# Attention and gated feed-forward on one core: constants as planned tasks, masks from five patterns, and new due times for the planner

## The chip, the cores and the metric

The kernel runs on one core of a Trainium2 chip. The core has TensorE (PE in the profile, with its weight loads as PEld), VectorE (DVE), ScalarE (ACT), GpSimd (POOL) and SyncE (SP, which here only issues DMAs). The metric is the device time of one launch in microseconds, the median of several runs.

## The reference

Eight batches, eight heads, 576 positions, head size 64. Heads 0 to 3 attend to the last 32 positions, heads 4 to 7 to every fourth position of the last 128. The result of all heads, 576 x 512 per batch, goes through a gated feed-forward with 1024 inner channels.

```python
scores = scale * np.matmul(q, k.transpose(0, 1, 3, 2))
rel = pos[:, None] - pos[None, :]
mask_plain = (rel >= 0) & (rel < window)                     # window 32
mask_dil = (rel >= 0) & (rel < window * dilation) & (rel % dilation == 0)   # dilation 4
...
attn = np.exp(scores - max) ; attn = attn / (sum + 1e-09)
x = matmul(attn, v)                       # heads side by side: (batch, 576, 512)
h = np.maximum(x @ w_in, 0.0)             # 512 -> 1024
conv_out = sum over k in 0..2 of conv_w[k] * h shifted by k - 1 along the sequence
gate = 1.0 / (1.0 + np.exp(-conv_out))
return h * gate @ w_out                   # 1024 -> 512
```

## The kernel before

**Attention.** Two heads make a pair; pairs 0 and 1 of a batch are plain, pairs 2 and 3 dilated. The scores of a pair are computed only inside the bands: 128 partitions by nine blocks of 64 columns, in three banks of a PSUM buffer called `att`, with 72 or 80 small matmuls (line 264). `att` has one buffer, used by a pair first for the scores (S) and later for the values (V, line 318). Between S and V stand on DVE and ACT: mask, maximum, exponential, sum, division, and a transpose to `pt` (line 307). After V, ACT writes the rounded result `xa` (line 368) and DVE the remainder `xb` (line 384); only then is `att` free.

**Eased pairs.** The eight pairs of batches 0 and 1 (`EASED = 8`) get their mask from TensorE: ahead of the scores three matmuls (line 253) with the weights `ones` (an identity in bf16) copy a mask from `mask_sb` to the three banks, and the scores are added on top. Then come a maximum on DVE (lines 274 to 278) and nine exponentials with sums on ACT (line 284). In later batches DVE adds the mask from `mask_sb` (lines 289 and 292), takes the maximum (294), subtracts it (296), ACT takes one exponential (298) and DVE sums (300).

**Masks.** `kinds_sb` holds five patterns of 64 columns, loaded by a DMA on ACT's queue. `mask_sb` holds for each kind ten blocks of 64 and is filled from the patterns by five ACT copies (lines 522 to 526). `ident` is an identity in fp32 that POOL makes; `minus` and `ones` are made from it by ACT (lines 516 and 517).

**Feed-forward.** A batch has a first product (line 402, into `mm`, and for half of batch 0's units into `nn`) in 16 units (eight chunks of 128 channels, two halves of 288 positions), each of four tasks of three matmuls (hi x hi, hi x lo, lo x hi). ACT applies the relu into `h` (line 409; three buffers), then the middle tap (420); DVE adds two taps (414), ACT takes the sigmoid (425), DVE multiplies (427), ACT rounds to `ga` (429) and DVE takes the remainder `gb` (431), the last gate step of a chunk. The second product (line 444, into `nn`) has eight units of eight tasks, one task for each chunk; ACT copies it out (451) and SP stores it.

**Weights.** They come as float64 and are turned into two fp32r parts by ACT and DVE (lines 477 to 512): an absolute value on ACT, five steps on DVE, and then either three matmuls on TensorE with `ident` and `minus` (lines 499 to 501, the nine "summed" ones) or two more DVE steps (506 and 512). POOL issues their DMAs (line 470) into the three buffers `out`.

**Order.** A planner written in Python sets the order of all engines when the kernel is built. Each piece of work is a task with an engine, a cost, a due time, the tasks it follows and the buffers it uses. The planner walks through time; of the tasks that could start within 0.25 of the earliest one on an engine it takes the one due first. The due times of attention pairs (`PAIR`), of first products, gates and second products (`DUE`) and of weights (`WI`, `WO`) are numbers; from batch 2 on they are those of one batch moved by `PERIOD`. The engines then run their instructions strictly in the planned order. What is set up before the planner (the mask DMA, the identity, the mask copies, the zeros at the edges of `h`) is not in the plan, and is put in order by the framework.

## Time and profile before

| what | value |
|---|---|
| median of 3 runs | 547.44 us (547.39 to 547.52) |
| profiled execution | span of 546.0 us from its first to its last instruction; the page gives no other time of it |
| PE busy | 514.2 us, 94% |
| DVE, ACT busy | 405.1 us (74%), 301.0 us (55%) |
| first matmul | at 9.96 us |
| granted TensorE clock, mean | 0.991 |

The busy time of matmuls is modelled at their ends, so a busy PE can still hold short waits. A row of the timeline gives start, duration, engine, line and instruction, with the idle time ahead of it and what ended it in brackets. A row of the waits gives the total, the number and the longest. Stages are given from the span's start. A unit's pace on PE is read from starts, not from the sum of durations, since matmuls overlap.

### The profile page before, as it was taken

How to read it: one execution, taken by the hardware profiler on the slowest of the kernel's cores; microseconds unless marked ns; L12 is line 12 of the kernel's file. 1: busy time of each engine (PE TensorE's matmuls, PEld its weight loads, DVE VectorE, ACT ScalarE, POOL GpSimd, SP SyncE). 2: the span in 40 equal slices, each digit the busy share in tenths (PEclk: the TensorE clock that was granted, in tenths of full speed). 3: DMA queues.
4: the chain of work that ended last, by engine and by line, in shares of the span. 5: the costliest groups of instructions: out<-in, count | busy, mean ns of one | idle time of the engine just before them, and what ended most of it. 6: DMA issues, size and time to landing. Idle time of an engine off the chain costs nothing.

```text
span 546.0 us, 18894 instructions
## 1 busy us (share of the span) xinstructions
PE 514.2 (94%) x8508; PEld 487.9 (89%) x8508; DVE 405.1 (74%) x692; ACT 301.0 (55%) x681; POOL 10.2 (2%) x29
## 2 busy tenths in 40 slices
PE   1668999999989999999999999999999999999997
PEld 1356888999979999999999999999999999999997
DVE  1878899998997389856998289856998289856920
ACT  3647799655742487237742577227743576237721
POOL 1100000000000000000000000000000000000000
PEclk9969999999999999999999999999999999999999
DMA  6656634022235102440045102440045102200011
GB/s 250 220 185 226 191 98 136 5 82 97 73 118 176 33 22 77 151 151 22 1 165 165 57 13 78 153 147 23 1 161 176 49 14 78 99 26 22 1 44 43
DMA packets 16959, 52.29 MB, mean 96 GB/s; under 512 B 1888, under 2 KB 3056, under 8 KB 16880
## 3 DMA queue, kind: packets, MB, share of 16 engines
q1 hardware_dynamic: 14400, 42.60, 23.7%
q0 software_dynamic: 2336, 8.41, 4.7%
q8 instruction: 66, 1.08, 0.8%
q10 hardware_dynamic: 144, 0.08, 0.1%
q14 instruction: 13, 0.11, 0.1%
HBM read 41.66 MB, written 9.44 MB: 94 GB/s over the span
## 4 chain that ended last, share of the span: by engine, by line
PE 80%; ACT 10%; DVE 7%; DMA 1%; issue 1%; POOL 0%; ACTq 0%; DVEq 0%; POOLq 0%
PE nn L444 36%; PE mm L402 32%; PE att L318 6%; PE att L264 5%; ACT s L284 4%; DVE c L414 2%; DMA out<-in_w_in_dram 1%; ACT c L420 1%; ACT h L409 1%; DVE m L274 1%; ACT c L425 1%; DVE c L427 1%; ACT L425 0%; DVE pt L307 0%; ACT w1a L477 0%
## 5 line engine op out<-in xcount | busy, mean ns | idle before, releaser
L414 DVE SCALAR_TENSOR_TENSOR c<-h,conv_sb,c 128x576 f32<-128x576 f32 x128 | 103.9, 815 | 37.8 <-ACT c L420 36.6
L409 ACT ACTIVATE h<-mm 128x288 f32<-128x288 f32 x120 | 48.9, 409 | 51.9 <-PE mm L402 51.7
L451 ACT COPY out<-nn 128x288 f32<-128x288 f32 x64 | 25.3, 398 | 71.0 <-PE nn L444 66.8
L427 DVE TENSOR_TENSOR c<-c,h 128x576 f32<-128x576 f32 x64 | 48.0, 754 | 14.4 <-ACT c L425 12.8
L318 PEld LDWEIGHTS att<-pt,v 32*64 32x64 f32 x2944 | 38.6, 135 | 14.7 <-ACT s L284 5.1
L318 PE MATMUL att<-pt,v 32*64 32x64 f32 (+2 forms) x2944 | 42.4, 230 | 8.4 <-ACT s L284 4.0
L420 ACT ACTIVATE c<-h,conv_sb 128x576 f32<-128x576 f32 x64 | 49.5, 775 | 1.1
L425 ACT ACTIVATE c<-c 128x576 f32<-128x576 f32 x64 | 43.4, 679 | 5.2 <-DVE c L414 4.4
L402 PE MATMUL mm<-x2a,wi 128*128 128x288 f32 x144 | 40.6, 297 | 0.7 <-ACT h L409 0.7
L402 PE MATMUL mm<-x0a,wi 128*128 128x288 f32 x144 | 40.4, 296 | 0.0
L402 PE MATMUL mm<-x3a,wi 128*128 128x288 f32 x144 | 40.3, 296 | 0.0
L402 PE MATMUL mm<-x1a,wi 128*128 128x288 f32 x144 | 40.3, 295 | 0.0
L444 PE MATMUL nn<-g0a,wo 128*128 128x288 f32 x128 | 37.3, 306 | 0.2
L264 PE MATMUL att<-qk 64*32 64x64 f32 x2432 | 35.4, 232 | 1.8 <-DVE s L292 1.4
L444 PE MATMUL nn<-g2a,wo 128*128 128x288 f32 x128 | 36.7, 302 | 0.0
L444 PE MATMUL nn<-g1a,wo 128*128 128x288 f32 x128 | 36.5, 300 | 0.0
L444 PE MATMUL nn<-g3a,wo 128*128 128x288 f32 x128 | 36.4, 299 | 0.0
L264 PEld LDWEIGHTS att<-qk 64*32 64x32 f32 x2432 | 29.7, 109 | 7.4 <-issue 4.1
L444 PE MATMUL nn<-g4a,wo 128*128 128x288 f32 x128 | 36.3, 299 | 0.0
L444 PE MATMUL nn<-g6a,wo 128*128 128x288 f32 x128 | 36.2, 299 | 0.0
L402 PE MATMUL mm<-x4a,wi 128*128 128x288 f32 x128 | 35.8, 295 | 0.0
L402 PE MATMUL mm<-x5a,wi 128*128 128x288 f32 x128 | 35.8, 295 | 0.0
(170 smaller groups left out, 1498.5 us busy)
## 6 DMA issues: line engine op xcount, KB each, us to landing
qk<-in_qk_d_dram SPq DMA_DIRECT2D x16, 664.0 KB, 4.7
qk<-in_qk_p_dram SPq DMA_DIRECT2D x16, 592.0 KB, 4.1
out_dram<-out SPq DMA_DIRECT2D x28, 288.0 KB, 2.1
v<-in_v_p_dram SPq DMA_DIRECT2D x16, 384.0 KB, 3.7
v<-in_v_d_dram SPq DMA_DIRECT2D x16, 384.0 KB, 3.5
out<-in_w_in_dram POOLq DMA_DIRECT2D x8, 512.0 KB, 4.0
out<-in_w_out_dram POOLq DMA_DIRECT2D x8, 512.0 KB, 3.9
out_dram<-out SPq DMA_DIRECT2D x8, 144.0 KB, 1.8
```

Source lines behind the costliest of these rows:

```text
L264: nc.tensor.matmul(sc.t[quad * 32:quad * 32 + 32, bank, c * W:c * W + W], q, k, start=i == 0 and not eased, stop=i == len(parts) - 1, skip ...
L274: last = plan.add("DVE", 0.68, due + 1.5, lambda: nc.vector.tensor_reduce(out=m.t.rearrange("p (h a) -> p h a", h=2)[:, :, 0:4], in_=banks ...
L284: nc.scalar.activation(out=s.t[:, i, :], in_=sc.t[:, bank, c * W:c * W + W], func=AF.Exp, scale=SCALE, bias=m.t[:, i:i + 1], accum_out=z.t ...
L318: nc.tensor.matmul(tv.t[hd * 64:hd * 64 + 64, bank, o:o + n], v.t[quad * 32:quad * 32 + 32, block // 2, block % 2 * 64:block % 2 * 64 + 64 ...
L402: nc.tensor.matmul(ps.t[:, 0:HALF], wi[jw][fc][:, k * 128:k * 128 + 128], x[k].t[jx][:, hf * HALF:hf * HALF + HALF], start=(k == 0 and i = ...
L409: relu.append(plan.add("ACT", 0.4, due + 1.6 * u + 1.6, lambda fc=fc, hf=hf, ps=ps: nc.scalar.activation(out=h[fc].t[:, 1 + hf * HALF:1 + ...
L414: nc.vector.scalar_tensor_tensor(out=c[fc].t, in0=h[fc].t[:, k:S + k], scalar=conv_sb[:, k, fc:fc + 1], in1=c[fc].t, op0=ALU.mult, op1=ALU ...
L420: t = plan.add("ACT", 0.777, d, lambda fc=fc: nc.scalar.activation(out=c[fc].t, in_=h[fc].t[:, 1:S + 1], func=AF.Copy, scale=conv_sb[:, 1, ...
L425: t = plan.add("ACT", 0.686, d + 1.0, lambda fc=fc: nc.scalar.activation(out=c[fc].t, in_=c[fc].t, func=AF.Sigmoid), [t], [c[fc]], "sigmoid")
L427: t = plan.add("DVE", 0.755, d + 1.5, lambda fc=fc: nc.vector.tensor_tensor(out=c[fc].t, in0=c[fc].t, in1=h[fc].t[:, 1:S + 1], op=ALU.mult ...
L444: nc.tensor.matmul(ps.t[:, 0:HALF], wo[jw][2 * dm + k // 4][:, k % 4 * 128:k % 4 * 128 + 128], g[k].t[jg][:, hf * HALF:hf * HALF + HALF], ...
L451: outs.append(plan.add("ACT", 0.4, out_due + 3.3 + 3.3 * u, lambda hf=hf, ps=ps, o=o: nc.scalar.copy(out=o.t[:, hf * HALF:hf * HALF + HALF ...
```

## The change

The constants become tasks of the plan with very early due times, and the mask copies tasks with due time 70 (`MASKS`); only the mask DMA stays ahead of the plan, as ACT's first instruction. The scores follow the task that makes `ones`. In eased pairs TensorE no longer reads `mask_sb`: it builds each bank from the patterns themselves, which it reads repeated. In the planner, engines begin at times of their own (`FIRST`) instead of 0, a load on SP takes 0.3 longer, and a first S 0.4 longer in batch 0. All due times are replaced, now with own numbers for every batch.

```diff
+DUE = {
+    0: (-0.8, 5.8, -44.0),
...
+}
+PAIR = {
+    0: (-206.5, -338.2, -201.8, -179.4),
+    1: (-72.2, -148.2, -76.5, -59.2),
...
+}
+MASKS = 70.0
...
-    LATENCY = {"DVE": 0.05, "ACT": 0.05, "SP": 2.0, ...
+    LATENCY = {"DVE": 0.05, "ACT": 0.05, "SP": 2.3, ...
+    FIRST = {"SP": 0.75, "POOL": 1.0, "PE": 4.5, "ACT": 2.5}
...
-        at = 0.0
+        at = self.FIRST.get(t.engine, 0.0)
...
-                for bank, (c0, c1) in enumerate(((0, 256), (320, 576), (256, 320))):
-                    nc.tensor.matmul(sc.t[:, bank, 0:c1 - c0], ones, mask_sb[:, kind, c0:c1], start=True, stop=True,
-                                     skip_group_check=True)
+                own = ((0, 1), (2, 3)), ((2, 4),), ((1, 1),)
+                if kind == 1:
+                    own = ((3, 1), (2, 3)), ((3, 1), (2, 3)), ((4, 1),)
+                for bank, runs in enumerate(own):
+                    c = 0
+                    for i, n in runs:
+                        nc.tensor.matmul(sc.t[:, bank, c * W:(c + n) * W].rearrange("p (a k) -> p a k", k=W), ones,
+                                         kinds_sb[:, i, :].unsqueeze(1).to_broadcast([128, n, W]),
+                                         start=c == 0, stop=True, skip_group_check=True)
+                        c += n
...
-        last = plan.add("PE", (0.8, 0.92)[kind] + (0.5 if eased else 0.0), due, scores, [lq], [qk, sc, s], "S")
+        last = plan.add("PE", (0.8, 0.92)[kind] + (0.5 if eased else 0.0) + (0.4 if b == 0 else 0.0), due, scores, [lq, made], [qk, sc, s], "S")
...
-    nc.scalar.dma_start(out=kinds_sb, in_=mask)
-    make_identity(nc, ident)
-    nc.scalar.mul(out=minus, in_=ident, mul=-1.0)
-    nc.scalar.copy(out=ones, in_=ident)
+    made = plan.add("POOL", 0.6, -1e4, lambda: make_identity(nc, ident))
+    made = plan.add("ACT", 0.29, -1e4, lambda: nc.scalar.copy(out=ones, in_=ident), [made])
+    plan.add("ACT", 0.29, -1e4, lambda: nc.scalar.mul(out=minus, in_=ident, mul=-1.0), [made])
...
+    masked = [None, None]
+    for kind, (rest, own) in enumerate(((0, lambda: nc.scalar.copy(out=slot_masks[0][:, 0:5:4, :], in_=kinds_sb[:, 0:2, :])),
+                                        (1, lambda: nc.scalar.copy(out=slot_masks[1][:, 0:6:5, :], in_=spread(3, 2))))):
+        masked[kind] = plan.add("ACT", 0.72, MASKS, lambda k=kind: nc.scalar.copy(out=slot_masks[k], in_=spread(2, 10)))
+        masked[kind] = plan.add("ACT", 0.29, MASKS, own, [masked[kind]])
...
     with tc.manual_schedule():
+        nc.scalar.dma_start(out=kinds_sb, in_=mask)
         for t in plan.order():
             t.run()
```

The change moves instructions on all engines. Three places matter here. The first is ACT at the program's beginning. Before:

```order
L522 COPY mask_sb<-kinds_sb 128x640
L524 COPY mask_sb<-kinds_sb 128x640
L523 COPY mask_sb<-kinds_sb 128x2x64
L525 COPY mask_sb<-kinds_sb 128x2x64
L526 COPY mask_sb<-kinds_sb 128x64
L477 ACTIVATE w0a<-out_151 128x512
L516 ACTIVATE minus<-ident 128x128
L517 CAST ones<-ident 128x128
L284 ACTIVATE s_104,z_110<-att_160,m_107 128x64 x9
```

The same place now:

```order
L531 COPY mask_sb<-kinds_sb 128x640 x2
L529 COPY mask_sb<-kinds_sb 128x2x64
L530 COPY mask_sb<-kinds_sb 128x2x64
L533 COPY mask_sb<-kinds_sb 128x64
L515 CAST ones<-ident 128x128
L516 ACTIVATE minus<-ident 128x128
L477 ACTIVATE w0a<-out_151 128x512
L284 ACTIVATE s_104,z_110<-att_160,m_107 128x64 x9
```

`ones` and `minus` have moved ahead of the first weight (`w0a`); the five mask copies still stand ahead of them.

The second place is TensorE at the program's beginning, where `qk` is a pair's queries and keys, `pt` its transposed weights. Before:

```order
L253 LDWEIGHTS ones
L253 MATMUL att_160<-mask_sb,ones 128x256
L253 LDWEIGHTS ones
L253 MATMUL att_160<-mask_sb,ones 128x256
L253 LDWEIGHTS ones
L253 MATMUL att_160<-mask_sb,ones 128x64
L264 MATMUL att_160<-qk_99 32x64 x36
```

The same place now:

```order
L251 LDWEIGHTS ones
L251 MATMUL att_160<-kinds_sb,ones 128x64
L251 LDWEIGHTS ones
L251 MATMUL att_160<-kinds_sb,ones 128x192
L251 LDWEIGHTS ones
L251 MATMUL att_160<-kinds_sb,ones 128x256
L251 LDWEIGHTS ones
L251 MATMUL att_160<-kinds_sb,ones 128x64
L264 MATMUL att_160<-qk_99 32x64 x36
```

A mask takes four matmuls (five for a dilated pair) instead of three, with the same columns. In the order of S and V turns, the batches 0 and 1 had S01 S02 S00 V01 V02 V00 S03 S11 V03 V11 S12 S13 V12 S10 V13 V10 (first digit the batch, second the pair); now it is S01 S00 V01 S02 V00 V02 S03 S11 V03 V11 S12 S10 V12 V10 S13 V13. From batch 2 on every batch had the same pattern, all S and V turns among the second product of the batch before; now each batch has its own, S41, S71 and S72 stand in or behind the first product of the batch before, V32, V33 and V63 in a first product, and S32, S33, S42, S63 and S73 one batch further ahead than they did.

The third place is DVE at the end of batch 1's gates, where `g5b`, `g6b` and `g7b` are the last gate steps of the last three chunks, and the `L289` and `L292` rows are the two reads of `att` with the mask in the first S turn of batch 2. Before:

```order
L431 TENSOR_TENSOR g5b<-c_149,g5a 128x576
L427 TENSOR_TENSOR c_150<-c_150,h_147 128x576
L414 SCALAR_TENSOR_TENSOR c_148<-h_145,conv_sb,c_148 128x576
L431 TENSOR_TENSOR g6b<-c_150,g6a 128x576
L414 SCALAR_TENSOR_TENSOR c_148<-h_145,conv_sb,c_148 128x576
L289 TENSOR_TENSOR s_106<-att_160,mask_sb 128x2x256
L427 TENSOR_TENSOR c_148<-c_148,h_145 128x576
L292 TENSOR_TENSOR s_106<-att_160,mask_sb 128x64
L294 TENSOR_REDUCE m_109<-s_106 128x9
L431 TENSOR_TENSOR g7b<-c_148,g7a 128x576
```

The same place now:

```order
L292 TENSOR_TENSOR s_106<-att_160,mask_sb 128x64
L294 TENSOR_REDUCE m_109<-s_106 128x9
L427 TENSOR_TENSOR c_149<-c_149,h_146 128x576
L414 SCALAR_TENSOR_TENSOR c_150<-h_147,conv_sb,c_150 128x576
L431 TENSOR_TENSOR g5b<-c_149,g5a 128x576
L414 SCALAR_TENSOR_TENSOR c_150<-h_147,conv_sb,c_150 128x576
L414 SCALAR_TENSOR_TENSOR c_148<-h_145,conv_sb,c_148 128x576
L427 TENSOR_TENSOR c_150<-c_150,h_147 128x576
L414 SCALAR_TENSOR_TENSOR c_148<-h_145,conv_sb,c_148 128x576
L431 TENSOR_TENSOR g6b<-c_150,g6a 128x576
L427 TENSOR_TENSOR c_148<-c_148,h_145 128x576
L296 TENSOR_TENSOR s_106<-s_106,m_109 128x576
```

The two reads of `att` have moved ahead of `g5b`. The step to `g7b` is the row after the last one shown, so `L292` stands twelve rows ahead of it instead of two.

More of the change, by code (lines that the diff above doesn't have):

```diff
@@ L57 @@
 SCALE = 1.0 / D ** 0.5
+DUE = {
+    0: (-0.8, 5.8, -44.0),
+    1: (92.2, 76.9, 392.9),
+    2: (-37.9, 28.2, 171.0),
+    3: (147.1, -10.2, 213.7),
+    4: (70.9, 182.0, 290.5),
+    5: (-14.9, 88.4, 335.8),
+    6: (241.1, 161.6, 380.2),
+    7: (274.4, 180.7, 438.1),
+}
+PAIR = {
+    0: (-206.5, -338.2, -201.8, -179.4),
+    1: (-72.2, -148.2, -76.5, -59.2),
+    2: (121.2, 152.9, 111.1, 119.9),
+    3: (165.4, 187.4, 155.3, 157.1),
+    4: (228.6, 195.4, 191.7, 218.2),
+    5: (251.4, 264.9, 280.0, 247.8),
+    6: (303.1, 303.5, 315.5, 283.1),
+    7: (397.3, 354.1, 355.5, 315.1),
+}
+WI = (-188.1, -90.2, -87.8, 2.3, -104.6, -2.5, -2.7, 3.1)
+WO = (23.7, 27.3, 24.3, 56.5, 41.4, 86.2, 142.2, 162.3)
+AHEAD = (8.0, 4.1, 0.0)
+MASKS = 70.0
 ONE = dict(start=True, stop=True, skip_group_check=True)
@@ L76 @@
 class Planner:
-    LATENCY = {"DVE": 0.05, "ACT": 0.05, "SP": 2.0, "POOL": 3.0, "E": 0.2, "S": 0.33, "T": 0.35, "V": 0.2}
+    LATENCY = {"DVE": 0.05, "ACT": 0.05, "SP": 2.3, "POOL": 3.0, "E": 0.2, "S": 0.33, "T": 0.35, "V": 0.2}
     OVERLAP = {"DVE": 0.08, "ACT": 0.095}
     GAP = 0.035
+    FIRST = {"SP": 0.75, "POOL": 1.0, "PE": 4.5, "ACT": 2.5}
     WINDOW = 0.25
@@ L196, in attn_moe @@
     slots("nn", 2, [128, 512], pool=psum)
-    DUE = {0: (-4.3, 1.8, 23.7), 1: (68.3, 34.2, 99.8)}
-    PAIR = {0: (-42.0, -47.4, -46.7, -32.4), 1: (-4.4, -28.5, -16.5, -5.9)}
-    WI, WO = (-21.6, -21.1, -2.7, -2.7, -3.0, -0.1, 7.2, 7.8), (10.5, 12.6, 37.1, 43.0, 43.8, 43.6, 51.6, 56.5)
-    AHEAD = (8.0, 4.1, 0.0)
-    PERIOD = 57.4
-    for b in range(2, B):
-        DUE[b] = tuple(t + PERIOD * b for t in (-5.3, 10.9, 32.3))
-        PAIR[b] = tuple(t + PERIOD * b for t in (-21.1, -18.7, -14.6, -13.5))
     SUMMED = 9
@@ L290, in attention @@
                 out=heads(flat()), in0=banks(), in1=heads(mask_sb[:, kind]), op=ALU.add),
-                [last], [sc, s])
+                [last, masked[kind]], [sc, s])
             last = plan.add("DVE", 0.215, due + 1.5, lambda: nc.vector.tensor_tensor(
@@ L512, in weights, with edges @@
         return step(0.53, [w], lambda: nc.vector.tensor_tensor(out=lo, in0=t(), in1=hi.bitcast(F32), op=ALU.subtract))
-    nc.scalar.dma_start(out=kinds_sb, in_=mask)
-    make_identity(nc, ident)
-    nc.scalar.mul(out=minus, in_=ident, mul=-1.0)
-    nc.scalar.copy(out=ones, in_=ident)
+    made = plan.add("POOL", 0.6, -1e4, lambda: make_identity(nc, ident))
+    made = plan.add("ACT", 0.29, -1e4, lambda: nc.scalar.copy(out=ones, in_=ident), [made])
+    plan.add("ACT", 0.29, -1e4, lambda: nc.scalar.mul(out=minus, in_=ident, mul=-1.0), [made])
+    def edges():
+        for h, in hs:
+            nc.gpsimd.memset(h[:, 0:1], 0.0)
+            nc.gpsimd.memset(h[:, S + 1:S + 2], 0.0)
+    plan.add("POOL", 0.4, -1e3, edges)
     spread = lambda i, n: kinds_sb[:, i, :].unsqueeze(1).to_broadcast([128, n, W])
     slot_masks = [mask_sb[:, kind, :].rearrange("p (a k) -> p a k", k=W) for kind in range(2)]
-    nc.scalar.copy(out=slot_masks[0], in_=spread(2, 10))
-    nc.scalar.copy(out=slot_masks[0][:, 0:5:4, :], in_=kinds_sb[:, 0:2, :])
-    nc.scalar.copy(out=slot_masks[1], in_=spread(2, 10))
-    nc.scalar.copy(out=slot_masks[1][:, 0:6:5, :], in_=spread(3, 2))
-    nc.scalar.copy(out=slot_masks[1][:, 4, :], in_=kinds_sb[:, 4, :])
-    for h, in hs:
-        nc.gpsimd.memset(h[:, 0:1], 0.0)
-        nc.gpsimd.memset(h[:, S + 1:S + 2], 0.0)
+    masked = [None, None]
[3 more added lines that the diff above has]
+        masked[kind] = plan.add("ACT", 0.29, MASKS, own, [masked[kind]])
+    masked[1] = plan.add("ACT", 0.24, MASKS, lambda: nc.scalar.copy(out=slot_masks[1][:, 4, :], in_=kinds_sb[:, 4, :]),
+                         [masked[1]])
     wired = [weights(w_in[c], 512, WI[c], pair=(wi[0][c], wi[1][c]), summed=c < SUMMED) for c in range(NF)]
```

## Prediction

> **What bounds the kernel now.** I read the page's totals first, then the busy time by stage, then TensorE's waits, and only then single rows.
>
> ```profile
> span 546.0 us, 18894 instructions
> ...
> 0.00:10.00 10.00, 0.04 (x1) 0.04 (x2) 0.00 (x0) 4.22 (x9) 2.60 (x15) 1.00 0.82 312
> 10.00:60.00 50.00, 37.17 (x1004) 27.50 (x1005) 39.25 (x90) 29.73 (x126) 4.33 (x8) 0.90 0.60 199
> 60.00:100.00 40.00, 37.42 (x644) 33.79 (x643) 37.62 (x70) 37.46 (x108) 1.58 (x3) 1.00 0.38 120
> 100.00:150.00 50.00, 50.00 (x443) 49.74 (x442) 46.85 (x76) 30.21 (x57) 1.70 (x3) 1.00 0.22 70
> 150.00:160.00 10.00, 8.31 (x194) 7.29 (x194) 9.61 (x18) 4.87 (x8) 0.00 (x0) 1.00 0.48 154
> 160.00:500.00 340.00, 339.25 (x5922) 328.45 (x5921) 252.42 (x417) 174.84 (x337) 0.00 (x0) 1.00 0.26 83
> ```
>
> The columns of a stage are its length and the busy us of PE, PEld, DVE, ACT and POOL. From 160 to 500 PE idles 0.75 us of 340: nothing to win there, only to lose. What can be won stands ahead of 160: 10.0 before the first matmul, 12.8 in the next 50, 2.6 in the next 40, 1.7 from 150 to 160. From 60 to 100 DVE and ACT are as full as PE, and DVE stays 94% full to 150. So the start is a chain through three engines, and the rest is PE's work alone. Who ends PE's waits (us in total, times, longest):
>
> ```profile
> PE att L253 <- ACT ones L517: 10.0, 1, 10.0
> PE att L253 <- ACT s L284: 6.7, 4, 4.0
> ...
> PE nn L444 <- DVE g7b L431: 0.6, 2, 0.4
> ```
>
> The longest wait is for one instruction of ACT, `ones`, which needs only `ident`:
>
> ```profile
> 5.24 0.72 ACT L522 COPY mask_sb<-kinds_sb 128x640 bf16<-128x640 bf16 x1 [2.79 <-DMA kinds_sb<-in_mask_dram]
> ...
> 6.89 0.24 ACT L526 COPY mask_sb<-kinds_sb 128x64 bf16<-128x64 bf16 x1
> 8.86 0.66 ACT L477 ACTIVATE w0a<-out 128x512 f32<-128x512 f32 x1 [1.73 <-DMA out<-in_w_in_dram]
> ...
> 9.62 0.28 ACT L517 CAST ones<-ident 128x128 bf16<-128x128 f32 x1
> ...
> 9.96 0.66 PE L253 MATMUL att<-mask_sb,ones 128*128 128x256 bf16 x3 [9.96 <-ACT ones L517]
> ```
>
> ACT stands at 8.86 on a weight, and `ones` stands behind it.
>
> **First term, the start.** In the new order `ones` stands ahead of the weight, but still behind the five mask copies: MASKS = 70 does not push them back, since the planner has ACT free from 2.5 and does not count their wait for the DMA. So PE does not start when `kinds_sb` lands (5.24), which masks from the patterns would allow. The copies end at 7.13; with the overlap of these rows `ones` runs from 7.04 to 7.32, and PE starts 0.07 later, at 7.39 instead of 9.96: **-2.57**. POOL now makes `ident` and the edges before it issues the first weight. That moves it by a few tenths (an estimate from the instructions put ahead), to a landing near 9.2 and an end of its ACT step near 9.9. Behind it wait the exponentials, which are ready 3.12 after the first matmul (13.08 less 9.96, next fence), at 10.5: not held.
>
> **Second term, masks by TensorE.** 24 pairs of weight load and matmul become 36 over the same 576 columns a mask: one more in a plain turn, two in a dilated one.
>
> ```profile
> L253 PEld LDWEIGHTS <-ones x24: 95/102/152, 10.0 to 73.5; 128*128 128x128 bf16 x24
> ...
> 13.08 0.31 ACT L284 ACTIVATE s<-att,m 128x64 f32<-128x64 f32 x1 [3.18 <-DVE m L278]
> ```
>
> One more pair costs between 0 (hidden under the matmul ahead) and 0.152, the longest load (ns, least/median/most). Nearest is the median, of which a part is hidden: 0.08, so 12 make **+1.0**, ends 0 and +1.8. By the Trainium skill's page TensorE: Matmul & The Clock Gate, section LDWEIGHTS, a load takes its columns over 1.2 GHz, 107 ns for these 128. The trace's median of 102 agrees; with every load paid in full, as that page's figure has it, the sum would be 0.3 worse.
>
> **Third term, the turns in `att`.** PSUM holds one `att`, and a pair needs it twice, for scores (S) and values (V), with DVE and ACT between. Below, S12 is the scores of batch 1, pair 2. Starts of turns now:
>
> ```profile
> 44.90 0.41 PE L253 MATMUL att<-mask_sb,ones 128*128 128x256 bf16 x3 [0.68 <-ACT s L284]
> 50.76 1.36 PE L318 MATMUL att<-pt,v 32*64 32x64 f32 x96 [1.45 <-ACT s L284]
> 53.77 0.77 PE L318 MATMUL att<-pt,v 32*64 32x32 f32 x50
> 57.42 0.42 PE L253 MATMUL att<-mask_sb,ones 128*128 128x256 bf16 x3
> 63.55 0.41 PE L253 MATMUL att<-mask_sb,ones 128*128 128x256 bf16 x3 [0.86 <-ACT s L284]
> 69.59 1.36 PE L318 MATMUL att<-pt,v 32*64 32x64 f32 x96 [0.40 <-ACT s L284]
> 73.37 0.42 PE L253 MATMUL att<-mask_sb,ones 128*128 128x256 bf16 x3
> 84.65 1.36 PE L318 MATMUL att<-pt,v 32*64 32x64 f32 x96 [0.52 <-ACT s L284]
> ...
> 250.83 19.08 PE mm L402 x144
> ```
>
> An S turn takes 5.9 (S11, from 44.90) to 6.1 (S12, from 57.42), a V turn 3.0 (V03, from 50.76) to 3.8 (V12, from 69.59); S10, from 73.37, takes 11.3, since ACT comes late to its exponentials. The new order is S01 S00 V01 S02 V00 V02 S03 S11 V03 V11 S12 S10 V12 V10 S13 V13. Laid end to end at these lengths, with 0.08 for each new pair, 0.7 more at V01 (PE sums a weight between it and S02) and 0.5 more at S03 (DVE is in a weight), S12 begins at 55.5, 1.9 ahead of 57.42, and S13, the last S, at 74.7. Behind S13 PE has 23 tasks of the first product (three matmuls each, 0.40 by the last row) to cover its exponentials, so the long turn costs PE nothing and it has all of batch 0's first product behind it near 88. Then DVE leads. From S12's maximum to batch 0's last gate it does now:
>
> ```profile
> 12.89 0.42 DVE L479 TENSOR_SCALAR w0a<-w0a 128x512 f32<-128x512 f32 x1
> ...
> 14.99 0.69 DVE L490 SCALAR_TENSOR_TENSOR r<-out,w0a 128x512 fp32r<-128x512 uint32 x1
> ...
> 59.67 0.69 DVE L274 TENSOR_REDUCE m<-att 128x8 f32<-128x512 f32 x1
> ...
> 89.90 0.69 DVE L512 TENSOR_TENSOR wo<-w0b,wo 128x512 fp32r<-128x512 f32 x1
> ...
> 104.39 0.75 DVE L431 TENSOR_TENSOR g7b<-c,g7a 128x576 fp32r<-128x576 f32 x1
> ...
> 107.74 0.30 PE L402 MATMUL mm<-x2a,wi 128*128 128x288 f32 x1
> ```
>
> That is 45.5, from 59.67 to 105.14. A weight costs DVE 2.8 in five steps (12.89 to 15.68), 4.0 with the two steps more that an unsummed one has (0.6 net each). Between the same two points stood 10.7 of weight steps, now 11.9; the rest is equal. So the gate is done 46.7 after the new maximum at 57.9: 104.6. As a mark I take the moment when PE has 36 tasks of the next stage behind it, which needs that gate in the new order: now 107.74, where the 37th begins, then 104.6 and one task with its delay, 105.2. That is -2.5 in all, so this term is **-0.9**; its ends are +1.0 (turns at their longest) and -2.4 more (DVE's idle in the stage from 60 to 100, all gone).
>
> **Fourth term, the last gate of batch 1.** PE now stands twice here:
>
> ```profile
> 152.63 0.97 PE L264 MATMUL att<-qk 64*32 64x64 f32 x72 [1.45 <-DVE s L292]
> 153.28 0.75 DVE L431 TENSOR_TENSOR g7b<-c,g7a 128x576 fp32r<-128x576 f32 x1
> ...
> 154.09 0.40 PE L444 MATMUL nn<-g7b,wo 128*128 128x288 f32 x1 [0.15 <-DVE g7b L431]
> ...
> L414 DVE SCALAR_TENSOR_TENSOR c<-h,conv_sb,c 128x576 f32<-128x576 f32 x128 | 103.9, 815 | 37.8 <-ACT c L420 36.6
> ```
>
> S21 waits for DVE's second read of S20, queued between gates; in the new order that read of S22 stands ten rows earlier, and S23 finds `att` free. From the mark PE has 106 tasks (42.1) and two S (2.5: the 0.97 of the first row and 0.3 of change between kinds of matmul, each) to the matmul on `g7b`: 149.8. DVE now takes 48.9 from the one gate (105.14) to the other (154.03). In the new order this stretch holds 17.9 of weight steps instead of 22.4, one tap more (0.815, the last row) and one attention step more (0.7): 45.9, so 150.5. PE passes at 150.5 instead of 154.09: -3.6 since the start, **-1.1** here, ends -0.7 more (PE's own 149.8) and +2 (one stall as now).
>
> **Small terms.** POOL's first weight in the chain of waits (from 1.44, 7.40 long); its second one and SP's third load in the list of issues (KB, us from issue to landing; they are issued at 2.43 and 1.64):
>
> ```profile
> 1.44 7.40 DMA out<-in_w_in_dram
> ...
> out<-in_w_in_dram POOLq DMA_DIRECT2D x1, 512.0 KB, 8.5
> ...
> v<-in_v_p_dram SPq DMA_DIRECT2D x1, 384.0 KB, 7.8
> ```
>
> PE visits V 32 times from the products instead of 30; the first matmul after a visit takes 0.40 (154.09) instead of 0.30 (107.74), and the entry about as much: **+0.4**. At the end one task of batch 6 stands between the last first product and the last second product, beside waits of 0.6 and more: **-0.4**. ACT's table loads stay 16. `ident` and the edges on POOL are hidden behind the wait for the mask patterns, to 5.24; without that cover they would cost a few tenths. On SP the second scores' load now stands third, behind a load of values; the third load now lands at 9.4, and S00 needs it at 13.4, so 0.
>
> **Sum:** -2.6 + 1.0 - 0.9 - 1.1 + 0.4 - 0.4 = -3.6, a span of 542.4. The median of the runs is 1.44 above the profiled span; kept, that gives 543.8.
>
> **Rivals.** *Attention now stands among gates* (slower). Now all S and V after batch 1 stand among the second product; in the new order S41, S71 and S72 stand in or behind the first product, where DVE has two taps of 0.815 and two steps of 0.7 in the gates of a chunk, 3.0, for 3.18 of PE (eight tasks), so 1.3 to spare in a batch. An S brings DVE six passes near the 0.75 of the gate row and some small steps, 5.1; what isn't spare keeps `h`, then `mm`, busy and stops PE: 3.8 each, 11 in all. Against it: tasks of the second product are kept back as fill there. It decides when more than a third is uncovered: over 4.7 lost. Half of it gives 549.4. 0.12.
> *The first weight lands late.* POOL's third transfer is now a weight and not the 24 KB of the convolution. If the first landed as late as the second does (10.9), the exponentials would move by 1.1: 544.9. By the Trainium skill's page DMA: Bandwidth & Descriptors, section Queues, rings and completion order, an engine goes round the queues packet by packet, so a later transfer of the same queue does not slow an earlier one; the order of landing here agrees. 0.12.
> *Only the start is won:* DVE idles as much as before and the stall at 152 stays: -1.6 with the masks at 1.0, -0.8 with them at 1.8: 545.8 to 546.6. 0.15.
> *More is won:* V turns at 3.0, masks mostly hidden, no stall at 150: -6.4, 541.0. 0.16.
>
> **How the numbers follow.** The forecast has 0.45. Faster or slower means by over 0.2%, 1.1 us, about what a measurement can tell: faster is 0.45 + 0.16 + 0.11 + 0.06 = 0.78, slower 0.11, the rest 0.11. The range, 541.2 to 547.2, takes in the three cases of a gain and leaves out the slow one and the far end of the best.
>
> **What would show it.** The first matmul near 7.4; 36 pairs at L251; S13 near 75; the last gate of batch 0 near 104.6, the matmul on the last gate of batch 1 near 150.5; PE idle under 1 us from 160 to 500. Wrong I am if PE stands in the first products of batches 3 and 6, or if the turns are much longer than now.

## The result, and the profile after

| kernel | median, us | runs | ratio to before |
|---|---|---|---|
| before | 547.48 (547.39 to 548.21) | 4 | |
| changed | 543.41 (542.00 to 544.81) | 4 | 0.9915 [0.9894, 0.9935] |

The change won 4.1 us by the medians, which is 0.74%, and 0.85% by the ratio, whose interval leaves out 1. The profiled execution of the changed kernel has a span of 540.6 us and a time of 542.39; the spans of its four runs are 540.2, 540.6, 542.6 and 543.0. A time stands 1.8 above its span. The two profiles are 5.4 apart, more than the medians, since this execution is one of the two shorter ones; the experiments show where two executions of one kernel part.

The stages of the changed kernel (length, busy us of PE, PEld, DVE, ACT and POOL with their instructions, granted clock of PE, busy share of DMA, GB/s), to be laid beside those of before:

```profile
0.00:10.00 10.00, 1.96 (x76) 1.45 (x76) 0.50 (x1) 4.25 (x9) 2.61 (x15) 1.00 0.82 308
10.00:60.00 50.00, 37.44 (x942) 27.21 (x943) 42.40 (x99) 32.34 (x133) 4.97 (x9) 0.90 0.64 215
60.00:100.00 40.00, 37.95 (x661) 35.33 (x660) 37.66 (x68) 37.91 (x107) 1.58 (x3) 1.00 0.33 107
100.00:150.00 50.00, 50.00 (x520) 49.47 (x519) 47.62 (x76) 29.85 (x56) 1.05 (x2) 1.00 0.24 78
150.00:160.00 10.00, 10.00 (x291) 9.30 (x289) 9.57 (x20) 3.90 (x9) 0.00 (x0) 1.00 0.43 138
160.00:500.00 340.00, 339.62 (x5768) 328.86 (x5768) 250.47 (x413) 178.71 (x340) 0.00 (x0) 1.00 0.25 80
```

PE has more work done ahead of 10, has no idle time left from 150 to 160, and idles 0.38 instead of 0.75 from 160 to 500. From 10 to 60 it idles as much as before (12.6), at the same mean clock of 0.90: this stage starts earlier, it did not become shorter. PE's waits (us in total, times, longest):

```profile
PE att L251 <- ACT ones L515: 7.5, 1, 7.5
PE att L318 <- ACT s L284: 7.5, 4, 3.0
PE att L251 <- ACT s L284: 6.5, 3, 4.0
...
PE nn L444 <- DVE g7b L431: 0.4, 1, 0.4
```

The first wait is 2.45 shorter. The start row by row, from the timeline (start, duration, engine, line, instruction, and in brackets the idle time ahead and what ended it):

```profile
7.16 0.29 ACT L515 CAST ones<-ident 128x128 bf16<-128x128 f32 x1
7.51 0.66 PE L251 MATMUL att<-kinds_sb,ones 128*128 128x64 bf16 x4 [7.51 <-ACT ones L515]
8.10 1.37 PE L264 MATMUL att<-qk 64*32 64x64 f32 x72
9.14 0.66 ACT L477 ACTIVATE w0a<-out 128x512 f32<-128x512 f32 x1 [1.48 <-DMA out<-in_w_in_dram]
...
10.63 0.31 ACT L284 ACTIVATE s<-att,m 128x64 f32<-128x64 f32 x1 [0.83 <-DVE m L278]
```

`ones` ends ACT's mask copies and no longer waits for the weight. The weight's step on ACT is over before the exponentials are ready; they wait 0.83 for DVE's maximum. The mask takes 0.59 from the first matmul to the scores (7.51 to 8.10), with four pairs of load and matmul where there were three. Last, the marks of the prediction: S12's maximum, the last gate of batch 0, the 37th task behind batch 0's first product, the last gate of batch 1 and the matmul on it:

```profile
58.26 0.68 DVE L274 TENSOR_REDUCE m<-att 128x8 f32<-128x512 f32 x1
...
104.01 0.75 DVE L431 TENSOR_TENSOR g7b<-c,g7a 128x576 fp32r<-128x576 f32 x1
105.23 0.29 PE L402 MATMUL mm<-x6a,wi 128*128 128x288 f32 x1
149.05 0.76 DVE L431 TENSOR_TENSOR g7b<-c,g7a 128x576 fp32r<-128x576 f32 x1
150.12 0.29 PE L444 MATMUL nn<-g7b,wo 128*128 128x288 f32 x1
```

From S12's maximum to batch 0's last gate DVE takes 46.5 (58.26 to 104.76; 46.7 in the prediction), and from there to batch 1's last gate 45.0 (to 149.81; 45.9 in the prediction).

### The profile page after: what moved, and what is told of

Its sections match the earlier page's. It is cut to its first block, busy times and chain, and to the rows that moved or that the text cites. A ratio compares the mean times of both kernels' runs of the same rounds, so it can differ in the third digit from the quotient of the medians.

```text
span 540.6 us, 18907 instructions
## 1 busy us (share of the span) xinstructions
PE 513.8 (95%) x8520; PEld 487.6 (90%) x8520; DVE 403.2 (75%) x692; ACT 303.0 (56%) x681; POOL 10.2 (2%) x29
## 4 chain that ended last, share of the span: by engine, by line
PE 84%; ACT 7%; DVE 7%; issue 1%; DMA 1%; ACTq 0%; DVEq 0%
PE nn L444 38%; PE mm L402 34%; PE att L318 7%; PE att L264 5%; ACT s L284 4%; DVE c L414 1%; DVE m L274 1%; DMA kinds_sb<-in_mask_dram 1%; PE nn L499 1%; DVE pt L307 0%; DVE s L305 0%; DVE c L427 0%; ACT c L420 0%; DVE w0b L484 0%; ACT c L425 0%
## 5 line engine op out<-in xcount | busy, mean ns | idle before, releaser
L402 PE MATMUL mm<-x1a,wi 128*128 128x288 f32 x176 | 49.7, 297 | 0.0
L402 PE MATMUL mm<-x6a,wi 128*128 128x288 f32 x160 | 45.5, 299 | 1.0 <-ACT h L409 1.0
L444 PE MATMUL nn<-g5a,wo 128*128 128x288 f32 x128 | 36.6, 301 | 0.0
L444 PE MATMUL nn<-g7a,wo 128*128 128x288 f32 x128 | 35.7, 298 | 0.0
```

Of the source, the lines that this page charges most:

```text
L402: nc.tensor.matmul(ps.t[:, 0:HALF], wi[jw][fc][:, k * 128:k * 128 + 128], x[k].t[jx][:, hf * HALF:hf * HALF + HALF], start=(k == 0 and i = ...
L444: nc.tensor.matmul(ps.t[:, 0:HALF], wo[jw][2 * dm + k // 4][:, k % 4 * 128:k % 4 * 128 + 128], g[k].t[jg][:, hf * HALF:hf * HALF + HALF], ...
```

## The experiments

Each kernel ran beside runs of the kernel before on one chip; ratios are to those. The marks are those above: first matmul, first mark (105.23 in the changed kernel), second mark (150.12), last matmul (536.97). A task is three matmuls of a product, counted from the first of the program; "at task 200" compares the starts of the task behind the first 200.

**1. `ones` behind the weight again.** Only this is undone:

```diff
-        for t in plan.order():
+        done = plan.order()
+        first = next(t for t in done if t.engine == "ACT" and t.due == WI[0])
+        done.remove(first)
+        done.insert(next(i for i, t in enumerate(done) if t.engine == "ACT" and t.due == -1e4), first)
+        for t in done:
```

> The changed kernel with one thing undone: on ACT the two constants made from ident stand again behind the first weight's absolute value; all else keeps its order. The weight's step ran from 9.14 to 9.80, so the first matmul should come near 10.0 instead of 7.51. Theory (the start is passed on whole, since the chain of turns, DVE and then PE hang on it): every mark moves by 2.5, span near 543.1, time near 545.9. Rival (DVE's weight steps, which do not hang on the first matmul, lead from 76 to 150 and take up part of the delay): the matmul on batch 1's last gate moves by 1 or less, time near 544.4.

Measured: 546.88, ratio 0.9965 [0.9949, 0.9982], by the ratios 0.50% or 2.7 us worse than the changed kernel. The place in the timeline:

```profile
9.52 0.66 ACT L477 ACTIVATE w0a<-out 128x512 f32<-128x512 f32 x1 [2.00 <-DMA out<-in_w_in_dram]
10.08 0.28 ACT L515 CAST ones<-ident 128x128 bf16<-128x128 f32 x1
10.42 0.66 PE L251 MATMUL att<-kinds_sb,ones 128*128 128x64 bf16 x4 [10.42 <-ACT ones L515]
```

The first matmul came 2.9 later, since the weight itself landed at 9.52 instead of 9.14. The marks came 4.5 later than in the changed kernel's first profile and 3.7 later than in its second (number 5). The start is passed on: nothing behind it absorbs it, as the rival had it. Why the marks moved by more than the 2.9 was not taken apart.

**2. The old due times in the changed kernel.** `DUE`, `PAIR`, `WI` and `WO` are those of before, with `PERIOD`; constants, masks and the planner's clock stay changed.

```diff
+    DUE = {0: (-4.3, 1.8, 23.7), 1: (68.3, 34.2, 99.8)}
+    PAIR = {0: (-42.0, -47.4, -46.7, -32.4), 1: (-4.4, -28.5, -16.5, -5.9)}
...
+    PERIOD = 57.4
```

> The changed kernel with the due times of before; the constants, the masks from patterns and the planner's clock stay. Theory (start 2.45, the rest from the order of turns and gates): the first matmul stays near 7.5, S10 is again the long last S turn, PE stands again at batch 1's last gate, time near 545.0. Rival (the due times matter little, the start is all there is): time within 0.5 of the changed kernel, near 543.4. Rival (old due times do not fit a clock that begins later): above 546.

Measured: 546.13, ratio 0.9965 [0.9948, 0.9982]. So the rest of the change alone is worth 0.35%, and the new tables 0.4 to 0.5% more (0.9915 and, in number 5, 0.9927 with them). Its marks and one of its waits:

```profile
105.93 0.30 PE L387 MATMUL mm<-x2a,wi 128*128 128x288 f32 x1
152.29 0.40 PE L429 MATMUL nn<-g7b,wo 128*128 128x288 f32 x1 [0.15 <-DVE g7b L416]
540.83 0.29 PE L429 MATMUL nn<-g7a,wo 128*128 128x288 f32 x1
...
PE att L249 <- DVE s L277: 1.4, 1, 1.4
```

| stretch, us | before | old due times | changed | changed, number 5 |
|---|---|---|---|---|
| to the first matmul | 9.96 | 7.42 | 7.51 | 7.67 |
| to the first mark | 97.78 | 98.51 | 97.72 | 98.36 |
| to the second mark | 46.35 | 46.36 | 44.89 | 44.90 |
| to the last matmul | 388.28 | 388.54 | 386.85 | 387.99 |

With the old tables the stretch between the marks and the last one are as long as before to 0.3, and the wait for DVE's second read of the scores (1.4) is back. The 1.5 between the marks belongs to the order that the tables give: that stretch is 44.9 in the profile of every kernel with the new tables but number 11. The last stretch is less firm. With the changed kernel's plan it is 387.0 in number 1, 386.7 in number 3, 388.0 in number 5 and 387.5 in number 6, so of the 1.4 in the first profile only some 0.3 is left in another execution.

**3. Masks from `mask_sb`, three matmuls each,** in the same plan:

```diff
-                for bank, runs in enumerate(own):
...
+                for bank, (c0, c1) in enumerate(((0, 256), (320, 576), (256, 320))):
+                    nc.tensor.matmul(sc.t[:, bank, 0:c1 - c0], ones, mask_sb[:, kind, c0:c1], start=True, stop=True,
```

> The changed kernel, same plan, but TensorE takes the masks of the eased pairs from mask_sb in three matmuls again instead of four or five from the patterns. Prediction's second term (0.08 for each of 12 pairs, in turns that PE waits for): 1.0 faster. Rival, from the trace after (four pairs took 0.59 from 7.51 to 8.10, as three did before, and five took 0.34): no change, within 0.3.

Measured: 544.22, ratio 0.9924 [0.9899, 0.995], the same as the changed kernel. These intervals are no narrower than the 1.0 in question, so the rows must decide. The first mask took 0.59 here too:

```profile
7.66 0.66 PE L246 MATMUL att<-mask_sb,ones 128*128 128x256 bf16 x3 [7.66 <-ACT ones L508]
8.25 1.06 PE L257 MATMUL att<-qk 64*32 64x64 f32 x55
```

And a dilated one at full clock, S03, first here with three pairs, then in the changed kernel with five:

```profile
37.52 0.42 PE L246 MATMUL att<-mask_sb,ones 128*128 128x256 bf16 x3
37.87 1.13 PE L257 MATMUL att<-qk 64*32 64x64 f32 x80
```

```profile
35.44 0.41 PE L251 MATMUL att<-kinds_sb,ones 128*128 128x64 bf16 x5
35.78 1.13 PE L264 MATMUL att<-qk 64*32 64x64 f32 x80
```

From the mask's start to the scores it is 0.35 with three and 0.34 with five. The twelve pairs more cost nothing.

**4. A first try at keeping PE warm.** Matmuls that nobody reads, 512 columns each, into the fourth bank of `att` behind the scores of five pairs.

```diff
+            for _ in range(WARM.get((b, p), 0)):
+                nc.tensor.matmul(sc.t[:, 3, :].rearrange("p (a k) -> p a k", k=W), ones,
+                                 kinds_sb[:, 2, :].unsqueeze(1).to_broadcast([128, 8, W]), **ONE)
```

> The changed kernel with 32 matmuls of 128x512 more, put behind the scores of pairs 01, 00, 02, 03 and 11 into a bank of att that scores leave free; their result is overwritten, so the output is the same. They fill waits of PE. Theory (PE's clock fell to 0.50 at 50 to 55 after the 3.0 wait ahead of V03, and that made V03's turn 4.6 long instead of 3.1): granted clock near 1.00 all through 10 to 60, V03's turn near 3.1, S12 near 54.8, and the times of its runs closer together than 542.0 to 544.8; time 1 to 2 lower. Rival (DVE leads behind S13, so earlier turns are waited away): the marks at 105 and 150 and the time stay. Rival (the added matmuls hold up what follows them): slower by up to 2.

Measured: 549.94, ratio 1.003 [1.0011, 1.0048], slower than before. The eight behind the first scores:

```profile
10.05 3.08 PE L269 MATMUL att<-kinds_sb,ones 128*128 128x512 bf16 x8
```

DVE's maximum over the scores began only behind them (13.16, with PE as what ended its wait): the buffer is one tile, and its reader waited for the last writer, though that one wrote another bank. The run tested that wait and not the clock. Number 7 does it in other buffers.

**5. The changed kernel once more,** beside the next three.

> The changed kernel once more, beside the other three, so that they are compared with it on one chip. Both theories: 543.4, about 4 us (0.7%) below the kernel before; first matmul at 7.5, batch 0's first product behind PE at 88.9, 36 tasks of the next stage at 105.2, the last matmul at 537.

Measured: 544.63 (543.6 to 545.21), ratio 0.9927 [0.9909, 0.9945]. Its profiled span is 542.5, 1.9 over the first profile of the same kernel. Of that 0.8 had come by task 200 of the products, 0.6 more by task 250, 0.5 more by task 750. The first part was there by S02, which began at 23.59 instead of 22.79. It is TensorE's speed: from its start to what follows it, V01 took 1.59 here (19.54 to 21.13) and 1.08 in the first profile (19.37 to 20.45). The granted clock in the rows does not show this. It reads 1.00 from 10 to 20 in both profiles, where the second mask takes 0.57 instead of 0.34 later on. Behind 24 both have stretches at a lower granted clock: 0.66 from 30 to 35 and from 50 to 55 here, 0.82 and 0.50 from 45 to 55 there. The second part is taken up in number 9.

**6. `ones` and `minus` ahead of the mask copies,** nothing else moved:

```diff
-        for t in plan.order():
+        tasks = plan.order()
+        for t in spots + [t for t in tasks if t not in spots]:
```

(`spots` are the tasks that make `ident`, `ones` and `minus`.)

> The changed kernel with ones and minus ahead of the five mask copies on ACT, and nothing else moved. Theory of the start: the masks of the eased pairs need only the patterns (landed at 5.36) and ones, so the first matmul comes at 5.4 instead of 7.5. ACT's exponentials of the first pair still stand behind the first weight, which lands at 9.1, so they begin at 9.7 instead of 10.6: of the lead of 2.1 only 0.9 is kept, S00 begins at 12.5 instead of 13.45, and all later marks and the end are 0.9 earlier, 542.5. Rival: the queries and keys of the first pair land later than the patterns, so the scores wait and less than 0.5 is won: 543.0 or more. Second rival: the rest of the start does not hang on the weight, and all 2.1 is won: 541.3.

Measured: 542.68, ratio 0.9901 [0.9878, 0.9925].

```profile
5.22 0.64 PE L251 MATMUL att<-kinds_sb,ones 128*128 128x64 bf16 x4 [5.22 <-DMA kinds_sb<-in_mask_dram]
8.94 0.66 ACT L477 ACTIVATE w0a<-out 128x512 f32<-128x512 f32 x1 [1.84 <-DMA out<-in_w_in_dram]
9.51 0.30 ACT L284 ACTIVATE s<-att,m 128x64 f32<-128x64 f32 x1
```

As the theory had it: the first matmul comes with the patterns, 2.3 earlier, and the exponentials stand right behind the weight, only 1.1 earlier (S00 at 12.3 for 13.45). The marks are 1.3 earlier, the last matmul 0.65 earlier than in the changed kernel's first profile and 2.6 earlier than in the second. By the medians it is 2.0 under number 5, by ratios 0.26%, about the size of the two intervals.

**7. PE kept busy in its waits, without a reader.** Nine such matmuls into `mm`, free at that time, behind the first scores, and 5, 11, 8 and 12 into `nn` ahead of four weight sums:

```diff
+WARM = {-188.1: 5, -90.2: 11, -2.7: 8, -2.5: 12}
...
             def add():
+                for _ in range(WARM.get(due, 0)):
+                    nc.tensor.matmul(ps.t.rearrange("p (a k) -> p a k", k=W), ones,
+                                     kinds_sb[:, 2, :].unsqueeze(1).to_broadcast([128, 8, W]), **ONE)
```

> The changed kernel with TensorE kept busy in its waits of the first 48 us: matmuls whose result nobody reads, of 512 columns in bf16, 9 into a free bank of mm behind the first scores, and 5, 11, 8 and 12 into nn ahead of the sums of the first, third, fifth and sixth weight. No other engine waits for them, since each sum's result is read only behind the next exponentials. Theory of the clock: the turn of V03 took 4.6 instead of 3.1 because TensorE came out of a wait of 3.0 at half its clock (granted 0.82 and 0.50 from 45 to 55). Then the granted clock is near 1.00 in every 5 us from 10 to 60, V03's turn takes 3.1, S12 begins at 54 to 55 instead of 56.5, and the marks and the end are 1 to 2 earlier: 541.4 to 542.4. Rival: DVE and ACT lead there. Then the turns move but the mark at 105.2 does not, and the time stays at 543.4. Second rival: the matmuls overrun the waits: 1 slower.

Measured: 542.67 (542.1 to 542.86), ratio 0.9892 [0.9874, 0.991]. First the changed kernel at V03, then this one (two stages and their rows each):

```profile
45.00:50.00 5.00, 2.29 (x97) 2.25 (x98) 4.27 (x9) 4.62 (x23) 0.53 (x1) 0.82 0.34 125
50.00:55.00 5.00, 5.00 (x96) 3.26 (x95) 3.61 (x8) 2.16 (x5) 0.53 (x1) 0.50 0.47 161
...
47.71 1.85 PE L318 MATMUL att<-pt,v 32*64 32x64 f32 x96 [3.03 <-ACT s L284]
49.50 2.07 PE L499 MATMUL nn<-w1b,ident 128*128 128x512 f32 x2
...
52.35 1.66 PE L318 MATMUL att<-pt,v 32*64 32x32 f32 x88
```

```profile
45.00:50.00 5.00, 4.47 (x107) 2.75 (x105) 4.46 (x9) 4.50 (x21) 0.53 (x1) 1.00 0.36 125
50.00:55.00 5.00, 4.76 (x185) 4.19 (x185) 4.83 (x12) 4.05 (x9) 0.64 (x1) 1.00 0.72 221
...
47.40 1.36 PE L323 MATMUL att<-pt,v 32*64 32x64 f32 x96 [0.53 <-ACT s L289]
48.70 1.13 PE L507 MATMUL nn<-w1b,ident 128*128 128x512 f32 x2
...
50.41 1.15 PE L323 MATMUL att<-pt,v 32*64 32x32 f32 x88
```

At a granted clock of 1.00 the V takes 1.36 instead of 1.85, the weight's sum 1.7 instead of 2.85, and V03's turn 3.0 instead of 4.6. S12 begins at 53.9 (56.5 in the changed kernel), its maximum comes at 55.4 (58.3), and the first mark at 102.4, 2.8 earlier. DVE's 46.5 from that maximum to the gate stay as they are; PE's clock sets when the maximum comes. From 20 to 25 the granted clock is still 0.66, in all other stretches of 5 us to 60 it reads 1.00. The Trainium skill's page TensorE: Matmul & The Clock Gate, Part 1: The HAM clock gate, says that after an idle window of about 3.4 us the array runs at half its clock, and that the window runs freely, so that cold stretches vary between runs. The trace agrees in part: a wait was followed by a stretch at 0.50, and two executions of one kernel had such stretches at other places; but that wait was 3.03, shorter than the page's figure, and no run here tests a threshold. The spread of the runs is 0.8, in number 5 it was 1.6; since it is 1.3 and 1.4 in numbers 8 and 12, which fill the same waits, it is not shown that the filling lowers it.

Yet the time is only 2.0 under number 5 (0.35% by the ratios), and the last matmul (537.1) no earlier than in the changed kernel's first profile. Task by task, the lead over that profile was 2.8 at task 200 and 0.2 at task 250; number 9 is about that.

**8. Both edits at once,** with 12 matmuls behind the first scores.

> Both edits at once, with 12 instead of 9 matmuls behind the first scores, since TensorE's first wait grows to 5.2. If start and clock are terms of their own, their gains add: 0.9 and 1 to 2, so 540.5 to 541.5. If DVE leads behind the start, 542.5 as with the first edit alone.

Measured: 541.74 (540.89 to 542.15), ratio 0.9874 [0.9855, 0.9893]. By the ratios this is 0.53% under number 5, where number 6 won 0.26% and number 7 0.35%: within the intervals the two gains add. The lead over the changed kernel's first profile was 3.4 at task 200 and 1.4 at task 250.

**9. Where the lead went: the loads.** Between tasks 200 and 250 the kernels stood in waits that no semaphore ended ("issue"). Number 7 with the loads of batches 2 and 3 cut to a sixth:

```diff
+        part = 6 if b in (2, 3) else 1
...
-            out=qk.t[:, :n], in_=(qk_p, qk_d)[kind][b, p % 2]), uses=[qk])
+            out=qk.t[:, :n // part], in_=(qk_p, qk_d)[kind][b, p % 2][:, :n // part]), uses=[qk])
```

> The kernel with TensorE kept busy (warm2), with the loads of queries, keys and values of batches 2 and 3 cut to their first sixth; their pairs then compute on stale numbers, with the same instructions in the same order. warm2 was 2.7 ahead of the changed kernel at its 200th task of the products (144.9 against 147.6) and had lost all of it by the 250th (177.6 against 177.7), in waits within attention turns that no semaphore ended, 0.9 and 1.3 long, where about 240 instructions of TensorE stand between the one and the other. Theory: these are waits for TensorE's own instructions, which come by DMA and are late because the loads of the next pairs keep the engines busy (57% from 165 to 178). Then with the loads cut the waits shrink under 0.5 in all, the lead of 2.5 to 2.7 is still there at task 250, and the time is 2 to 2.5 under warm2's 542.7: 540.2 to 540.7. Rival: the instructions come late whatever the loads do (the turns stand too close together): the waits stay at 2 or more, and so does the time, 542.7.

Measured: 542.22, ratio 0.9885 [0.9865, 0.9904], as number 7. PE's waits from 150 to 180, first of number 7, then of this kernel, and what the load queue took from 150 to 178 here (packets, MB, share of the DMA engines):

```profile
PE nn L449 <- issue: 1.3, 1, 1.3
PE att L265 <- issue: 0.9, 1, 0.9
```

```profile
PE att L266 <- issue: 0.9, 2, 0.7
PE nn L450 <- issue: 0.7, 1, 0.7
...
q1 hardware_dynamic: 1584, 1.58, 18.1%
```

The queue's share fell from 54% to 18%, the waits from 2.2 to 1.6, and of a lead of 2.45 at task 200 there was 0.3 left at task 250. The waits did not fall under 0.5, the lead went all the same, and the time did not move: the theory of the loads fell.

**10. Its control,** the same cut in the changed kernel.

> The changed kernel with the same cut of the loads of batches 2 and 3, the control of the run before. The changed kernel waited 0.2 in such turns in one profiled execution and 1.2 in another. Theory of the loads: 0 to 1 is won, 542.5 to 543.5 by the changed kernel's 543.4, and the lead of the warm kernel over this one is 2.5, as at task 200. Rival: 543.4 to 544.6, and the two kernels with cut loads differ by 1 or less.

Measured: 543.16, ratio 0.991 [0.9889, 0.9931], as the changed kernel. The two kernels with cut loads differ by 0.9 in the median, as the rival had it. From task 200 to 250 it lost 1.0 against the first profile, more than number 5 (0.6) with all its loads.

**11. The new due times in the kernel before.**

> The kernel before with the new due times and nothing else of the change (the planner's clock, the masks, the constants stay as they were). Theory: the numbers fit one plan on one clock; with other arrival times the same numbers give another order, and the planner's own end goes from 532 to 553. So clearly slower than before, by 2 to 4%: 558 to 570. Rival: the tables carry their part of the gain alone, 2 to 4 us: 543.5 to 545.5.

Measured: 580.09 (two runs), ratio 1.058 [1.0548, 1.0613], worse than expected. The tables are no property of the work: in a plan with other arrival times the same numbers give another order, with a wait for an output copy of 8.5 that the kernel before does not have.

**12. The borders of the instruction stream.** The waits of number 9 stood at fixed places. Here are those of number 8:

```profile
169.12 0.71 PE L265 MATMUL att<-qk 64*32 64x64 f32 x46
170.22 0.58 PE L265 MATMUL att<-qk 64*32 64x64 f32 x34 [0.40 <-issue]
...
172.12 1.10 PE L323 MATMUL att<-pt,v 32*64 32x32 f32 x85
174.32 0.30 PE L323 MATMUL att<-pt,v 32*64 32x32 f32 x3 [1.11 <-issue]
```

Between the two waits stand 34 score matmuls, three tasks (9 matmuls) and 85 matmuls of V: 128, each with its weight load, so 256 instructions. In numbers 7 and 9 it is 31, 9 and 88: 256 again. PE has 8520 loads and 8520 matmuls in the changed kernel, 66.6 times 256, and its DMA view lists 67 transfers of instructions (queue, number, MB, share):

```profile
q8 instruction: 67, 1.10, 0.8%
```

So PE's instructions seem to come in pieces of 256 (1.10 MB by 67 is 16.4 KB, 64 bytes each). The last kernel is number 8 with 256 instructions more than the changed kernel, so that the borders fall where the changed kernel has them:

```diff
-            for _ in range(12 if (b, p) == (0, 1) else 0):
+            for _ in range(7 if (b, p) == (0, 1) else 0):
...
+            for _ in range(85 if (b, p) == (0, 1) else 0):
+                nc.tensor.matmul(mms[0][0][0:32, 0:W], ones[0:64, 0:32], kinds_sb[0:64, 2, :], **ONE)
```

> The kernel with both edits (first_warm), in which the matmuls that nobody reads are now 128 instead of 48: 7 of 512 columns and 85 small ones (32 rows of 64 columns) behind the first scores, the others as before. So TensorE gets 256 instructions (128 weight loads, 128 matmuls) more than the changed kernel, where first_warm got 96 and the kernel with warm waits alone 90. The waits that no semaphore ended stood at fixed places of the program: in the changed kernel's repetition and with ones first in the scores behind task 240, 24 pairs of load and matmul before their end; with 90 instructions more in the scores behind task 243, 31 pairs before their end, 164 instructions further; with 96 more 3 pairs earlier. Theory: TensorE's instructions come in pieces of 256 (16 KB by the trace's transfers of instructions), the next piece is late where attention turns stand close, and what is lost hangs on where the borders fall: a program longer by 90 has them 90 earlier in the work, or 166 later. Then 256 more put the border back in the scores behind task 240, 24 pairs before their end, the loss from task 200 to 250 falls from 1.9 to about 0.6, and the time from 541.7 to 540.4. Rival: it hangs on how dense the turns are, not on borders: the waits stay where first_warm had them, and the time at 541.7. Second rival: the small matmuls overrun the first wait: 0.5 to 1 slower.

Measured: 539.70 (539.41 to 540.8), ratio 0.985 [0.9833, 0.9866].

```profile
167.16 0.79 PE L265 MATMUL att<-qk 64*32 64x64 f32 x56
168.45 0.48 PE L265 MATMUL att<-qk 64*32 64x64 f32 x24 [0.50 <-issue]
...
q8 instruction: 68, 1.11, 0.9%
```

The wait is back in the scores behind task 240, 24 matmuls before their end, as in number 5; the loss from task 200 to 250 is 0.7 instead of 1.9, and there is one transfer more. The first mark is 0.5 later than in number 8 (102.3 for 101.9), about as the second rival says. This is the fastest kernel of the study, 0.65 to 0.8% under the changed one by the ratios. Against number 8 the ratios differ by 0.24%, no more than their intervals, so the borders are shown by the places and not by the time.

That the waits hang on the borders of pieces of 256 instructions is shown by the traces of all kernels. Twelve of the fourteen have waits of this kind of over 0.2, 33 in all. Where such a wait ends, the loads and matmuls listed since the start leave nearly the same remainder by 256 in every kernel: 172 to 178 among the first 3,100 matmuls, 154 to 156 near the 5,900th, 146 near the 7,100th, 140 near the 8,000th. It falls slowly with the place, as it would if a few instructions that the trace doesn't list were fetched along.

Why a piece comes late can be read from the transfers of queue q8. In number 8 they run from 167.76 to 168.92 and from 171.94 to 172.87; PE goes on at 170.22 and 174.32, 1.3 and 1.45 behind their ends. In all 33 cases it is 1.1 to 1.5, and the next transfer starts 1.0 to 1.8 behind the border. With about 1.0 for a transfer that makes 3.1 to 4.3 from border to border (an estimate from these numbers; 4.1 from 170.22 to 174.32, with the wait). Where attention turns use up 256 instructions in less, PE waits, with the loads cut too. What makes up the two delays is open, and no run changed them.

## Why the prediction was right

The median (543.8 forecast, 543.4 measured) was met, and so were three parts of the mechanism: the start, DVE's way from S12's maximum through both last gates, and no stretch behind that gives it back. Two terms were not, and that the median came within 0.4 is in part luck. Term by term, from the changed kernel's two profiles, with the experiment that bears on it:

| term of the sum | forecast | first profile | number 5 |
|---|---|---|---|
| the start | -2.57 | -2.45 (9.96 to 7.51) | -2.29 |
| masks by TensorE | +1.0 | 0 (0.59 as before; number 3) | 0 |
| turns in `att`, to the first mark | -0.9 | -0.06 | +0.58 |
| last gate of batch 1 | -1.1 | -1.46 (number 2) | -1.45 |
| visits of V and the end | 0.0 | -1.43 | -0.29 |
| span | -3.6 | -5.4 | -3.5 |

**The start** came out by its steps: `ones` at 7.16 behind the copies, PE soon after, the weight landing at 9.14. That it is kept to the end was an assumption of the sum; number 1 shows it. The rival that the first weight lands late fell: the exponentials waited for DVE.

**The masks** are the term that was sized worst. Its lower end, 0, was right and the middle was taken. The first mask takes 0.59 with three pairs and with four, and a dilated one took 0.34 with five (35.44 to 35.78). The added loads of 0.1 are hidden, behind the matmuls of 64 columns too (the next one starts 0.03 behind such a matmul), and the columns in all did not change. By the Trainium skill's page TensorE: Matmul & The Clock Gate, section LDWEIGHTS, a load takes its columns over 1.2 GHz, an estimate of 107 ns here; with 12 of them paid in full, as the prediction weighed it, the term would have been further off still.

**The turns** were forecast 0.9 shorter and were not: -0.06 in the first profile, +0.58 in number 5, and 1.4 to 1.5 longer than before in numbers 1 and 3 (99.3 and 99.2). With the masks the forecast was +0.1, so in the first profile two misses of 0.9 cancel, which is luck. What failed is the length of one turn. V03 was taken at 3.0 from a row at full clock, and took 4.6, at 0.50. The prediction laid turns end to end at lengths of before, and a length of before holds a clock. In number 7, at 1.00, the turn is 3.0 and S12, forecast at 55.5, begins at 53.9.

That DVE leads behind S12's maximum, as the prediction says, held. S12 came 1.0 late, its maximum 0.4 late (58.3 for 57.9), with one tap ahead of it on DVE instead of two, and the gate 0.2 late (104.8 for 104.6). From that maximum to the gate DVE takes 46.5 in all eleven profiles of kernels with the new tables and the rest of the change, whatever came ahead, and 45.5 in the two with the old tables, before and number 2. So what is won ahead of S12's maximum reaches the gate whole.

**The gate of batch 1** came at 149.8 and the matmul on it at 150.1 (150.5 forecast); S20 at 150.87 finds `att` free and waits for nothing. From gate to gate DVE takes 45.0 to 45.1 in the same eleven profiles, where 45.9 was forecast, and 48.9 in the two with the old tables; with those the stretch between the marks is as long as before to 0.01.

**Behind it** the sum had +0.4 and -0.4. Measured is -1.43 in the first profile and -0.29 in number 5, so most of the 1.43 goes with the execution, and is not shown to come from the change. PE's idle time from 160 to 500, 0.75 before, is 0.38 in the first profile and 1.35 in number 5, where the waits of number 12 come in. The rest was not taken apart.

**The rivals.** Attention among the gates did not bite: PE idles 0.38 and 1.35 of 340, where this rival asks for over 4.7. "Only the start is won" is what number 2 gives, 546.13 where the kernel before took 548.41 beside it. The rest of that forecast, 0.8 to 1.6 won, was too low: it had the masks at 1.0 to 1.8, and number 2 won 1.9 by its ratio. "More is won" has the right span for the first profile (540.6) but not the median, since the span of one execution is 2 us or so from that of another. The gap of 1.44 that was added to the span came out as 2.8 against the first profile; that hid the 1.8 by which its span was missed. Against number 5's profile the span (542.4 forecast, 542.5 measured) is met, with the misses of the single terms as in the table.

## What to carry to other kernels

Read a duration together with the granted clock of its stage before it is used as a price elsewhere, and beside the same instruction in another place, since the clock in the rows read 1.00 here where matmuls took 0.57 instead of 0.34. A start that held every engine was passed on here to the end; look for what a first instruction really needs, and give it the first place on its queue. Number 6 shows the limit: of 2.3 at the first matmul 1.3 was kept, since the exponentials then waited behind the weight. Due times fit one plan and one clock; they can't be judged or reused apart from it, so weigh a change of tables by its order alone, stretch by stretch. When a gain is there at one mark and gone at the next, compare task by task: here it went in two waits that no semaphore ended. When several engines lead in turn, find the stretch that is as long in every profile (here DVE's 46.5): what is won ahead of it is kept, and its own length is changed by the order alone.
